# u transposed in pairs on the vector engine and gathered by SBUF copies, in place of TensorE transposes, in a windowed attention followed by a token mixer and an MLP

## The chip, the cores and the metric

The kernel runs on one core of one Trainium2 chip. The metric is device microseconds of one execution. The engines are TensorE (PE; its weight loads are shown as PEld), VectorE (DVE), ScalarE (ACT), GpSimd (POOL) and SyncE (SP). Inputs are float32 in HBM; the kernel works in bfloat16 with float32 sums and returns float32.

## What is computed

```python
def _attn_ref(q, k, v):                      # q, k, v: (8, 8, 576, 64)
    scores = scale * np.matmul(q, k.transpose(0, 1, 3, 2))
    rel = pos[:, None] - pos[None, :]
    mask = (rel >= 0) & (rel < 64)
    scores = np.where(mask, scores, -1000000000.0)
    ...                                      # softmax over the last axis
    return np.matmul(attn, v)

def _moe_ref(x, U, V, w_ch1, w_ch2):         # x: (8, 576, 512), U: (576, 32), V: (32, 576)
    xt = x.transpose(0, 2, 1)
    h = xt @ U @ V
    u = x + h.transpose(0, 2, 1)
    ch = np.maximum(u @ w_ch1, 0.0) @ w_ch2  # 512 -> 2048 -> 512
    return u + ch
```

x is the attention's output with the 8 heads side by side. Per batch the attention, then the low-rank mixing along the sequence, then an MLP for each token.

## The kernel before

The 8 x 576 = 4608 tokens are 36 tiles of 128 tokens. The MLP works on nine chunks of four tiles (512 tokens). The attention and the mixing work by batch (576 tokens, four and a half tiles), so a tile on the border of two batches gets its halves from both.

A hand-written schedule sets the order on every engine. Batch 0 is computed alone at the start. Then, for chunk c, `mlp(c)` gives 32 fills: 16 times `ch1` (four matmuls of 128x512 of the first MLP layer, into PSUM tile `psA`, then a ReLU on ScalarE or, for the five in `DVE_RELU`, on VectorE) and 16 times `ch2` (four matmuls of the second layer into `psU`; every fourth ends a tile, VectorE adds u to give `osb`, and SP's queue stores it). `psA` and `psU` share three PSUM banks. After each fill the work of batch b = c + 1 that is listed for that slot is issued. The lists `PLACE` (batches 3 to 7), `PLACE_1` and `PLACE_2` (batches 1 and 2) give the slots:

- `KT`: VectorE transposes raw Q and K in blocks of 32 (`kt`, `qt`). For batches 0 to 2 it moves pairs of bfloat16 as one 32-bit word; for later batches each element is loaded twice, and single elements are moved. In chunk c they are those of batch b + 1 from batch 3 on.
- `VC`: VectorE copies V shifted by 64 tokens (`vB` from `vA`, `pair_v`).
- `S`: scores of a sixth of the batch (`sc`), Exp on ScalarE (`pts`), the mask on VectorE.
- `PV`: attention times V for one tile (`xr`), normalised by VectorE into `xs`.
- `U`, `V`: the two mixing products. `hh` is copied by ScalarE, `psv` is added to x by VectorE and gives the tile `un` of u.
- `UT`: four TensorE transposes of a tile of u against the identity into a PSUM tile `tpu` (or `tpw`), and one copy into the chunk's transposed tile `uTc`, on ScalarE, for two tiles of batch 1 on VectorE. `uTc` is the moving operand of `ch1`.

For chunk 0 the transposed u is made in PSUM instead (`XT`, `UP`: transposes of x plus the mixing product) and cast by two copies each on ScalarE and VectorE.

`S`, `PV`, `U`, `V` (and `tpw`) take turns in two double PSUM banks (`ps_big`). Loads from HBM are all issued by POOL, in the order of the program: `load_w1`, `load_w2`, `load_kq(b)` (four issues for paired batches, eight for the others), `load_v(b)` (five). POOL is not tied to the chunks: it goes on as soon as the buffers are free. Q and K of batch 4 are issued from slot 5 of chunk 1, those of batches 5 to 7 at the start of chunks 2 to 4, and each needs its raw buffer read by the transposes of two batches before.

Of the kernel before, what the change touches and what calls it, by code (L numbers as in the profile page):

```python
# [8 lines left out]
ACT = mybir.ActivationFunctionType  # L9
ALU = mybir.AluOpType  # L10

BF16 = mybir.dt.bfloat16
FP32 = mybir.dt.float32
# [3 lines left out]
def kernel(  # L17
# [11 lines left out]
    nc = tc.nc  # L29
    B, H, S, D = q.shape  # L30
    DM = H * D
    R = moe_U.shape[1]
    F = moe_w_ch1.shape[1]
    P = nc.NUM_PARTITIONS
# [12 lines left out]
    CH = 512  # L47
# [13 lines left out]
    u_pool = ctx.enter_context(tc.tile_pool(name="un", bufs=14))  # L61
    c1_pool = ctx.enter_context(tc.tile_pool(name="c1", bufs=1))
    wk_pool = ctx.enter_context(tc.tile_pool(name="wk", bufs=2))
    out_pool = ctx.enter_context(tc.tile_pool(name="osb", bufs=4))
    ps_big = ctx.enter_context(tc.tile_pool(name="ps_big", bufs=2, space=bass.MemoryType.PSUM))
    first = ExitStack()
# [8 lines left out]
    NT = 5  # L75
    ident = const.tile([P, P], BF16, name="ident")
    mask = const.tile([P, 2 * NB, W], BF16, name="mask")
    w1b = const.tile([P, NDC, F], BF16, name="w1b")
    w2b = const.tile([P, NFC, DM], BF16, name="w2b")
    ub = [const.tile([P, NT, R], BF16, name=f"ub{i}") for i in range(2)]  # L80
    vrep = const.tile([P, W + S + W], BF16, name="vrep")
    bias = const.tile([P, 12, W], BF16, name="bias")
    idle = const.tile([P, CH], BF16, name="idle")
    xs = [const.tile([P, NT, H, D], BF16, name=f"xs{i}") for i in range(2)]
    vA = [const.tile([P, NFULL, H, VW], BF16, name=f"vA{i}") for i in range(2)]
# [102 lines left out]
    )  # L188
    nc.vector.tensor_copy(out=bias[:, NB:12, :], in_=bias[:, 6:NB, :])

    w1v = moe_w_ch1.rearrange("(c p) n -> p c n", p=P)
    w2v = moe_w_ch2.rearrange("(i p) m -> p i m", p=P)

    def load_w1(lo, hi):
        nc.gpsimd.dma_start(out=w1b[:, :, lo:hi], in_=w1v[:, :, lo:hi])

    def load_w2(lo, hi):
        nc.gpsimd.dma_start(out=w2b[:, lo:hi, :], in_=w2v[:, lo:hi, :])
# [11 lines left out]
    u_tiles = {}  # L210
    uT_tiles = {}

    def uT_of(c):
        if c not in uT_tiles:
            uT_tiles[c] = uT_pool.tile([P, NDC, CH], BF16, name="uTc")
        return uT_tiles[c]


    def attention(b, alone=False):
# [43 lines left out]
        def VC(ts, copy):  # L263
            def f():
                pair_v(b, ts, copy)
            return f
# [174 lines left out]
        def UT(t):  # L441
            def f():
                g = g0 + t
                wide = b == 1 and t % 2 == 1
                if wide:
                    tpb = ps_big.tile([P, 2, 2 * CH], BF16, name="tpw", tag="big")
                    tp = tpb[:, 0, 0:CH].rearrange("p (c q) -> p c q", q=P)
                else:
                    tp = psum["tp"].tile([P, NDC, P], BF16, name="tpu", tag="tp")
                for dc in range(NDC):  # L450
                    nc.tensor.transpose(  # L451
                        tp[:, dc, :], u_tiles[g][:, dc * P : (dc + 1) * P], ident[:]
                    )
                col = (g % TPC) * P
                copy = dve_copy if wide else nc.scalar.copy
                copy(out=uT_of(g // TPC)[:, :, col : col + P], in_=tp[:])  # L456
            return f

        pcs["KT"] = [KT(x, n) for n in range(NJ if pair else NJJ) for x in "kq"]
        pool_copy, dve_copy = nc.gpsimd.tensor_copy, nc.vector.tensor_copy  # L460
        if alone:
            pcs["VC"] = [
                VC(slice(t, t + 1), dve_copy if t < 3 else pool_copy) for t in range(NFULL)
            ]
        else:
            pcs["VC"] = [VC(slice(0, NFULL), dve_copy)]
        pcs["S"] = [SC(n) for n in ((0, 3, 1, 4, 2, 5) if pair else range(NPC))]

        def XT(t):
            def f():  # L470
                for dc in range(NDC):
                    nc.tensor.matmul(
                        xT0[dc // 2][:, dc % 2, t * P : (t + 1) * P],
                        x[:, t, 2 * dc : 2 * dc + 2, :].rearrange("p h d -> p (h d)"),
                        ident[:],
                        start=(t == 0),
                        stop=False,
                    )
            return f

        def UP():
            for dc in (0, 2, 1, 3):
                nc.tensor.matmul(
                    xT0[dc // 2][:, dc % 2, :],
                    hh["sb"][:, dc * P : (dc + 1) * P],
                    vrep[:, W : W + CH],
                    start=False,
                    stop=True,
                )
            for dc in (0, 2, 1, 3):  # L490
                copy = dve_copy if dc // 2 else nc.scalar.copy
                copy(out=uT_of(0)[:, dc, :], in_=xT0[dc // 2][:, dc % 2, :])  # L492

        pcs["XT"] = [XT(t) for t in range(NFULL)]
        pcs["UP"] = UP
        pcs["PV"] = [PV(t) for t in range(NT)]
        pcs["U"] = [UM((t,)) for t in range(NT)] if alone else [UM(tuple(range(NT)))]
        pcs["V"] = [VM((0, 1)), VM((2, 3)), VM((4,))]
        pcs["UT"] = [UT(t) for t in range(NT if odd else NT - 1)]
        return pcs  # L500


    DVE_RELU = (1, 4, 7, 10, 13)

    def mlp(c):
        uTc = uT_of(c)
        c1 = [None] * NFC

        def ch1(i):
            def f():  # L510
                ps = psum["mm"].tile([P, CH], FP32, name="psA", tag="mm")
                for dc in (0, 2, 1, 3) if c == 0 else range(NDC):
                    nc.tensor.matmul(  # L513
                        ps[:],
                        w1b[:, dc, i * P : (i + 1) * P],
                        uTc[:, dc, :],
                        start=(dc == 0),
                        stop=(dc == NDC - 1),
                    )
                c1[i] = c1_pool.tile([P, CH], BF16, name=f"c1_{i}")  # L520
                if i in DVE_RELU:
                    nc.vector.tensor_relu(out=c1[i][:], in_=ps[:])  # L522
                else:
                    nc.scalar.activation(out=c1[i][:], in_=ps[:], func=ACT.Relu)  # L524
            return f

        acc = {}

        def ch2(t, quarter):
            def f():  # L530
                g = c * TPC + t
                if quarter == 0:
                    acc[t] = psum["mm"].tile([P, DM], FP32, name="psU", tag="mm")
                for i in range(4 * quarter, 4 * quarter + 4):
                    nc.tensor.matmul(  # L535
                        acc[t][:],
                        c1[i][:, t * P : (t + 1) * P],
                        w2b[:, i, :],
                        start=(i == 0),
                        stop=(i == NFC - 1),  # L540
                    )
                if quarter == 3:
                    osb = out_pool.tile([P, DM], FP32, name="osb")
                    nc.vector.tensor_tensor(  # L544
                        out=osb[:], in0=acc[t][:], in1=u_tiles[g][:], op=ALU.add
                    )
                    nc.sync.dma_start(out=outf[g * P : (g + 1) * P, :], in_=osb[:])
            return f

        order = [(t, r) for t in range(TPC) for r in range(4)]  # L550
        if c == 0:
            order = [(t, r) for r in range(4) for t in range(3)] + [(3, r) for r in range(4)]
        return [ch1(i) for i in range(NFC)] + [ch2(t, r) for t, r in order]


    PLACE = {
        "VC": [0],
        "S": [1, 1, 4, 4, 7, 7],
        "PV": [10, 10, 13, 13, 15],
        "KT": [8, 9, 11, 12, 14, 15, 16, 18],  # L560
        "U": [17],
        "V": [19, 20, 22],
        "UT": [21, 22, 23, 24, 25],
    }
    PLACE_1 = {
        "KT": [13, 14, 15, 16],
        "S": [16, 16, 18, 18, 20, 20],
        "VC": [21],
        "PV": [23, 23, 25, 25, 26],
        "U": [28],  # L570
        "V": [29, 30, 31],
        "UT": [30, 31, 31, 32, 32],
    }
    PLACE_2 = {
        "KT": [1, 2, 3, 4],
        "S": [5, 5, 8, 8, 11, 11],
        "VC": [9],
        "PV": [14, 14, 16, 16, 18],
        "U": [20],
        "V": [22, 23, 24],  # L580
        "UT": [24, 25, 26, 27, 28],
    }
    KT_3 = [19, 20, 21, 23, 25, 27, 29, 30]
    KT_4 = [11, 12, 14, 16, 18, 19, 22, 25]


    def turn_over(n, cols=CH, to=None):
# [67 lines left out]
    for c in range(NCH):  # L655
# [13 lines left out]
        if b < B:  # L669
            if b == 1:  # L670
                load_kq(2)
            if b + 1 < B:
                load_v(b + 1)
            if b + 2 < B and b > 2:
                load_kq(b + 2)
            if b == 2:
                slots[5].append(lambda: load_kq(4))
            if b == 1:
                slots[23].append(lambda: load_kq(3))
            where = {1: PLACE_1, 2: PLACE_2}.get(b, PLACE)  # L680
            if b <= 2:
                place(b, ("KT",), where)
            place(b, ("VC", "S", "PV"), where)
            if 3 <= b + 1 < B:
                place(b + 1, ("KT",), {2: {"KT": KT_3}, 3: {"KT": KT_4}}.get(b, PLACE))
            place(b, ("U", "V", "UT"), where)
        for fill, extra in zip(mlp(c) + [lambda: None], slots):
            fill()
            for f in extra:
# [31 lines left out]
```

## Time and profile before

| | |
|---|---|
| time, median of 3 runs | 331.26 us (329.37 to 332.1) |
| profiled execution | 330.28 us, its span 328.6 us |
| granted TensorE clock | 0.998 |
| TensorE busy | 318.5 us, 97% of the span, 2949 matmuls |
| VectorE, ScalarE, POOL busy | 195.1, 118.3, 83.0 us |
| transposes of u on TensorE (line 451) | 128, of which 120 into `tpu` |
| copies of `uTc` from them (line 456) | 30 on ScalarE, 586 ns each; 2 on VectorE |
| HBM read, written | 48.94 MB, 9.44 MB |

The span runs from the first to the last instruction; the execution's time is 1.7 us more. A line such as `L451` is line 451 of the kernel. A group of instructions is shown as the output tile, an arrow and the inputs, with count, busy time, mean duration, and the idle time of the engine before it with what ended it. The mean duration of a matmul includes its way through the array; matmuls of 512 columns start 0.216 us apart when they follow each other. In the timeline a line has the start, the busy time, the engine, the line of code, the operation and the number of instructions, and in brackets the idle time before it with what ended it. In tables by stretch, an engine's busy time stands before the number of its instructions.

### The profile page before, as it was taken

The page shows a single profiled execution, that of the slowest core. Times are in us where ns is not written, and L with a number is a line of the kernel's source. Part 1 is how long each engine was busy: PE and PEld are TensorE (multiplying, and loading weights), DVE is VectorE, ACT ScalarE, POOL GpSimd, SP SyncE. Part 2 cuts the span into 40 slices and gives each one's busy share as a digit, 9 for nine tenths or more (in the row PEclk, how much of TensorE's full clock was granted, in tenths as well). Part 3 has the DMA queues.
Part 4 walks back from the last instruction along what each step waited for, and adds up shares of the span by engine and source line. Part 5 has one row for each costly group of instructions (what it writes and reads, how often), then busy time and mean ns, then how long its engine had stood idle before and what let it go on. Part 6 is the DMA issues. An engine that isn't in the chain of part 4 may idle for free.

```text
span 328.6 us, 6914 instructions
## 1 busy us (share of the span) xinstructions
PE 318.5 (97%) x2949; PEld 156.3 (48%) x2949; DVE 195.1 (59%) x339; ACT 118.3 (36%) x188; POOL 83.0 (25%) x112
## 2 busy tenths in 40 slices
PE   8989989899999999999999999999999999999995
PEld 8544444454454545454544454445445444444442
DVE  7654759588787885689457955696456512212211
ACT  1524350365027423552246233732182224203400
POOL 8571419554626226125501400000000000000000
PEclk9999999999999999999999999999999999999999
DMA  7999999999999997999991911001100010021011
GB/s 120 156 199 209 206 137 173 206 197 141 170 189 180 181 111 96 203 105 63 176 225 13 73 64 67 1 2 55 75 2 0 34 66 30 2 89 39 2 64 64
DMA packets 96573, 34.34 MB, mean 105 GB/s; under 512 B 86688, under 2 KB 89888, under 8 KB 96544
## 3 DMA queue, kind: packets, MB, share of 16 engines
q0 software_dynamic: 91360, 24.48, 83.8%
q1 hardware_dynamic: 5184, 9.44, 8.3%
q8 instruction: 23, 0.38, 0.5%
q14 instruction: 6, 0.05, 0.1%
HBM read 48.94 MB, written 9.44 MB: 178 GB/s over the span
## 4 chain that ended last, share of the span: by engine, by line
PE 79%; DMA 12%; DVE 5%; POOL 2%; issue 1%; ACT 0%; DVEq 0%
PE psU L535 36%; PE psA L513 32%; DMA vA<-in_v_dram 7%; DMA kr<-in_k_dram 5%; PE xr L375 3%; PE sc L341 3%; PE psv L420 2%; PE tpu L451 2%; PE pshh L401 1%; DVE un L431 1%; POOL vA L124 1%; DVE xs L385 1%; DVE kt L243 0%; DVE qt L243 0%; DVE osb L544 0%
## 5 line engine op out<-in xcount | busy, mean ns | idle before, releaser
L535 PE MATMUL psU<-w2b,c 128*128 128x512 bf16 x576 | 135.1, 379 | 0.0
L513 PE MATMUL psA<-uTc,w1b 128*128 128x512 bf16 x576 | 131.4, 379 | 0.9 <-DVE uTc L492 0.6
L524 ACT ACTIVATE c<-psA 128x512 bf16<-128x512 f32 x99 | 59.3, 599 | 100.2 <-PE psA L513 99.6
L513 PEld LDWEIGHTS <-w1b 128*128 128x128 bf16 x576 | 53.9, 98 | 63.9 <-issue 1.7
L535 PEld LDWEIGHTS <-c 128*128 128x128 bf16 x576 | 53.6, 98 | 60.2 <-issue 3.0
L544 DVE TENSOR_TENSOR osb<-psU,un 128x512 f32<-128x512 f32 x36 | 24.8, 690 | 64.0 <-PE psU L535 63.9
L522 DVE TENSOR_SCALAR c<-psA 128x512 bf16<-128x512 f32 x45 | 30.8, 685 | 34.8 <-PE psA L513 34.6
L124 POOL DMA_DIRECT2D vA<-in_v_dram x32 | 28.4, 892 | 62.2 <-PE xr L375 19.8
L349 ACT ACTIVATE pts<-sc 128x768 bf16<-128x768 f32 x42 | 31.8, 808 | 11.8 <-PE sc L341 10.0
L456 ACT COPY uTc<-tpu 128x512 bf16<-128x512 bf16 x30 | 17.6, 586 | 40.3 <-PE tpu L451 40.3
L356 DVE TENSOR_TENSOR pts<-pts,mask 128x768 bf16<-128x768 bf16 x42 | 23.1, 557 | 12.2 <-ACT pts L349 9.3
L431 DVE TENSOR_TENSOR un<-psv,xs 128x512 bf16<-128x512 f32 (+1 forms) x40 | 25.7, 682 | 7.0 <-PE psv L420 6.8
L385 DVE TENSOR_TENSOR xs<-xr,rcp 128x512 bf16<-128x512 f32 (+1 forms) x40 | 27.6, 691 | 1.4
L112 POOL DMA_DIRECT2D kr<-in_k_dram x20 | 16.6, 828 | 21.8 <-DVE kt L243 8.8
L375 PEld LDWEIGHTS <-pts 128*64 128x64 bf16 x576 | 12.4, 110 | 10.4 <-DVE xs L385 5.2
L112 POOL DMA_DIRECT2D qr<-in_q_dram x20 | 16.5, 826 | 3.0 <-DMA vA<-in_v_dram 1.1
L243 DVE STREAM_TRANSPOSE kt<-kr 128x576 bf16<-128x576 bf16 x20 | 16.0, 799 | 0.0
L243 DVE STREAM_TRANSPOSE qt<-qr 128x576 bf16<-128x576 bf16 x20 | 15.7, 787 | 0.0
L375 PE MATMUL xr<-vB,pts 128*64 128x65 bf16 x320 | 15.4, 196 | 0.3 <-DVE vB L137 0.2
L341 PEld LDWEIGHTS <-kt 64*64 64x64 bf16 (+1 forms) x720 | 10.1, 105 | 10.8 <-issue 10.4
L410 ACT CAST hh<-pshh 128x512 bf16<-128x512 f32 x8 | 4.7, 586 | 28.9 <-PE pshh L401 28.9
L341 PE MATMUL sc<-qt,kt 64*64 64x128 bf16 (+3 forms) x720 | 12.9, 215 | 1.8 <-issue 1.4
(64 smaller groups left out, 161.8 us busy)
## 6 DMA issues: line engine op xcount, KB each, us to landing
out_dram<-osb SPq DMA_DIRECT2D x36, 256.0 KB, 2.0
kr<-in_k_dram POOLq DMA_DIRECT2D x26, 288.0 KB, 10.4
qr<-in_q_dram POOLq DMA_DIRECT2D x26, 288.0 KB, 11.4
vA<-in_v_dram POOLq DMA_DIRECT2D x32, 128.0 KB, 7.2
w2b<-in_moe_w_ch_dram POOLq DMA_DIRECT2D x2, 1024.0 KB, 19.2
w1b<-in_moe_w_ch_dram POOLq DMA_DIRECT2D x2, 512.0 KB, 9.6
w1b<-in_moe_w_ch_dram POOLq DMA_DIRECT2D x1, 1024.0 KB, 10.6
vB<-in_v_dram POOLq DMA_DIRECT2D x8, 64.0 KB, 7.8
```

Of the source, the lines that this page charges most:

```text
L112: nc.gpsimd.dma_start(out=dst[32 * part : 32 * (part + 1), off : off + NJJ * RD].rearrange("p (n x) -> p n x", x=r * D), in_=src[b, m * NJ ...
L124: nc.gpsimd.dma_start(out=va[:, t, :, 0:D], in_=v[b, :, t * P : (t + 1) * P, :].rearrange("h p d -> p h d"),)
L243: nc.vector.transpose(out=dst[:, n * S : (n + 1) * S].rearrange("q (m p e) -> q m e p", p=32, e=r), in_=src[:, 32 + n * RD : 32 + (n + 1) ...
L341: nc.tensor.matmul(sc[half * W : (half + 1) * W, g, (a - lo) * W : (z - lo) * W], operand("k", g, jj, e, kb * W, (kb + 1) * W), operand("q ...
L349: nc.scalar.activation(out=dst, in_=sc[:, :, 0 : PB * W].rearrange("p g (n w) -> p g n w", w=W), func=ACT.Exp, scale=scale,)
L375: nc.tensor.matmul(xr[r0 : r0 + W, h // 4, (h % 4) * VW : (h % 4 + 1) * VW], pts[:, g, jj * NB + blk, :], rhs, start=True, stop=True,)
L385: nc.vector.tensor_tensor(out=x[lo:hi, t, :, :].rearrange("p (a h) d -> p a h d", a=2), in0=xv[:, :, :, 0:D], in1=rcp[lo:hi].to_broadcast( ...
L431: nc.vector.tensor_tensor(out=u_tiles[g][rs, :], in0=ps[rs, n, :], in1=xt[n][rs], op=ALU.add)
L513: nc.tensor.matmul(ps[:], w1b[:, dc, i * P : (i + 1) * P], uTc[:, dc, :], start=(dc == 0), stop=(dc == NDC - 1),)
L522: nc.vector.tensor_relu(out=c1[i][:], in_=ps[:])
L524: nc.scalar.activation(out=c1[i][:], in_=ps[:], func=ACT.Relu)
L535: nc.tensor.matmul(acc[t][:], c1[i][:, t * P : (t + 1) * P], w2b[:, i, :], start=(i == 0), stop=(i == NFC - 1),)
```

## The change

- For chunks 2 to 8, u is no longer transposed by TensorE. `TR` transposes a tile of u on VectorE, in 32x32 blocks of 32-bit words (pairs of bfloat16), into a staging tile `stg`. `gather` copies `stg` to `uTc` with 16 DMAs of 32 KB from SBUF to SBUF, eight on ScalarE's queue and eight on SP's. Batch 1 keeps `UT` for four tiles (chunk 1).
- `uTc` now holds pairs: contraction index, then token, then the two halves of a pair. So the rows of `w1b` are loaded in that order (two DMAs for each `load_w1`), `ch1` reads every second element of `uTc`, from chunk 2 on in runs of 32 tokens, and `XT`, `UP` and `UT` take every second column of x, `hh` and u.
- Q and K of batches 4 to 7 are loaded by `next_loads`: after the gather of chunk c + 1 (c = 1 to 4) POOL copies one element of each of the last two gathered pieces to `hold`, and then issues `load_kq(c + 3)`.
- V of batch 1 is paired tile by tile (`VC` in four parts).
- The first two `psA` of chunk 0 are taken from `ps_big`.
- The slot lists change: in `PLACE` and `PLACE_2` scores, PV, U and V stand earlier; `KT_4` is gone.

The core of the diff:

```diff
-    w1b = const.tile([P, NDC, F], BF16, name="w1b")
+    w1b = const.tile([P, 2, 2, F], BF16, name="w1b")
+    hold = const.tile([P, 2], BF16, name="hold")
...
     def load_w1(lo, hi):
-        nc.gpsimd.dma_start(out=w1b[:, :, lo:hi], in_=w1v[:, :, lo:hi])
+        for g in range(2):
+            nc.gpsimd.dma_start(out=w1b[:, g, :, lo:hi], in_=w1v[g, :, :, lo:hi])
...
-            uT_tiles[c] = uT_pool.tile([P, NDC, CH], BF16, name="uTc")
+            uT_tiles[c] = uT_pool.tile([P, 2, CH, 2], BF16, name="uTc")
...
-        if alone:
+        if b < 2:
             pcs["VC"] = [
-                VC(slice(t, t + 1), dve_copy if t < 3 else pool_copy) for t in range(NFULL)
+                VC(slice(t, t + 1), pool_copy if alone and t == 3 else dve_copy)
+                for t in range(NFULL)
             ]
...
-        pcs["UT"] = [UT(t) for t in range(NT if odd else NT - 1)]
+        pcs["UT"] = [UT(t) for t in range(NT - 1)] if b == 1 else []
...
+    def TR(g):
+        def f():
+            c, t = divmod(g, TPC)
+            if c not in stages:
+                stages[c] = stg_pool.tile([P, 8, TPC, 32, 2], BF16, name="stg")
+            nc.vector.transpose(
+                out=stages[c][:, :, t, :, :].rearrange("p j q e -> p j (q e)").bitcast(U32),
+                in_=u_tiles[g].bitcast(U32).rearrange("p (j x) -> p j x", x=32),
+            )
...
+    def next_loads(c):
+        def f():
+            for n in (14, 15):
+                i, j = (n + n // 4) % 4, n % 4
+                rows = slice(32 * j, 32 * (j + 1))
+                nc.gpsimd.tensor_copy(
+                    out=hold[rows, 0:1], in_=uT_of(c + 1)[rows, 0, i * TPC * 32, 0:1]
+                )
+            load_kq(c + 3)
...
+    def gather(c):
+        def f():
+            run = TPC * 32
+            for n in range(16):
+                i, j = (n + n // 4) % 4, n % 4
+                queue = nc.sync if n % 2 else nc.scalar
+                queue.dma_start(
+                    out=uT_of(c)[32 * j : 32 * (j + 1), :, i * run : (i + 1) * run, :].rearrange(
+                        "p g n e -> p g (n e)"
+                    ),
+                    in_=stages[c][32 * i : 32 * (i + 1)].rearrange(
+                        "p (g j) t q e -> p g j (t q e)", g=2
+                    )[:, :, j, :],
+                )
...
+        def uT_cols(dc):
+            cols = uTc[:, dc // 2, :, dc % 2]
+            if c < 2:
+                return cols
+            return cols.rearrange("p (i t q) -> p t i q", i=4, t=TPC)
...
+                if c == 0 and i < 2:
+                    ps = ps_big.tile([P, 2, CH], FP32, name="psA0", tag="big")[:, 0, :]
...
     PLACE = {
-        "VC": [0],
-        "S": [1, 1, 4, 4, 7, 7],
-        "PV": [10, 10, 13, 13, 15],
-        "KT": [8, 9, 11, 12, 14, 15, 16, 18],
-        "U": [17],
-        "V": [19, 20, 22],
-        "UT": [21, 22, 23, 24, 25],
+        "VC": [2],
+        "S": [0, 0, 3, 3, 6, 6],
+        "PV": [9, 9, 11, 11, 13],
+        "KT": [14, 15, 16, 17, 22, 23, 25, 26],
+        "U": [15],
+        "V": [17, 18, 20],
     }
     PLACE_1 = {
         "KT": [13, 14, 15, 16],
-        "S": [16, 16, 18, 18, 20, 20],
-        "VC": [21],
-        "PV": [23, 23, 25, 25, 26],
-        "U": [28],
-        "V": [29, 30, 31],
-        "UT": [30, 31, 31, 32, 32],
+        "S": [16, 16, 18, 18, 21, 21],
+        "VC": [20, 21, 22, 23],
+        "PV": [22, 22, 24, 25, 26],
+        "U": [27],
+        "V": [28, 28, 29],
+        "UT": [29, 30, 31, 31],
     }
     PLACE_2 = {
-        "KT": [1, 2, 3, 4],
-        "S": [5, 5, 8, 8, 11, 11],
-        "VC": [9],
-        "PV": [14, 14, 16, 16, 18],
-        "U": [20],
-        "V": [22, 23, 24],
-        "UT": [24, 25, 26, 27, 28],
+        "KT": [0, 0, 1, 2],
+        "S": [2, 2, 5, 5, 8, 8],
+        "VC": [7],
+        "PV": [11, 11, 13, 13, 15],
+        "U": [17],
+        "V": [19, 20, 22],
     }
-    KT_3 = [19, 20, 21, 23, 25, 27, 29, 30]
-    KT_4 = [11, 12, 14, 16, 18, 19, 22, 25]
+    KT_3 = [16, 18, 19, 20, 24, 25, 27, 29]
...
-            if b + 2 < B and b > 2:
-                load_kq(b + 2)
-            if b == 2:
-                slots[5].append(lambda: load_kq(4))
...
+        if 2 <= c + 1 < NCH:
+            g0 = (b * S) // P
+            first = (c + 1) * TPC
+            last = max(first + t - g0 for t in range(TPC)) // 2 if b < B else 0
+            ready = where["V"][last] if b < B else 6
+            for t in range(TPC):
+                slots[ready - 1 + t // 2 if t < TPC - 1 else ready + 1].append(TR(first + t))
+            slots[ready + 1].append(gather(c + 1))
+            if c > 0 and c + 3 < B:
+                slots[ready + 1].append(next_loads(c))
```

In chunk 1 `ready` is slot 20, in chunk 2 slot 18, in chunks 3 to 6 slot 17, in chunk 7 slot 6.

## Prediction

> **What bounds the kernel now.** I read the busy shares first, then the chain, then the groups that the change touches.
>
> ```profile
> PE 318.5 (97%) x2949; PEld 156.3 (48%) x2949; DVE 195.1 (59%) x339; ACT 118.3 (36%) x188; POOL 83.0 (25%) x112
> DMA  7999999999999997999991911001100010021011
> PE psU L535 36%; PE psA L513 32%; DMA vA<-in_v_dram 7%; DMA kr<-in_k_dram 5%; PE xr L375 3%; PE sc L341 3%; PE psv L420 2%; PE tpu L451 2%; PE pshh L401 1%; DVE un L431 1%; POOL vA L124 1%; DVE xs L385 1%; DVE kt L243 0%; DVE qt L243 0%; DVE osb L544 0%
> L456 ACT COPY uTc<-tpu 128x512 bf16<-128x512 bf16 x30 | 17.6, 586 | 40.3 <-PE tpu L451 40.3
> ```
>
> TensorE is the bound: whatever leaves it in the middle of a chunk is gained, as long as nothing else becomes late. VectorE and ScalarE have room. The DMA engines are full for the first 22 slices (180 us) and nearly empty afterwards. The DMA shares of the chain lie in chunk 0, where TensorE was working beside them.
>
> The timeline of chunk 1 gives the price of one transposed tile:
>
> ```profile
> 92.92 1.03 PE L535 MATMUL psU<-w2b,c 128*128 128x512 bf16 x4
> ...
> 93.78 0.39 PE L451 MATMUL tpu<-ident,un 128*128 128x128 bf16 x4
> ...
> 94.00 1.03 PE L535 MATMUL psU<-w2b,c 128*128 128x512 bf16 x4
> ```
>
> Starts count, not durations: four transposes push the next start from 93.78 to 94.00, 0.22 us.
>
> **What is removed.** 28 of 32 groups of four transposes: 27 in chunks 1 to 6, between back-to-back matmuls, 27 x 0.22 = **-5.9 us**; one in chunk 0 (counted there). 28 ScalarE copies of 0.586 us go too, worth nothing by themselves.
>
> **Chunk 0.** Three waits of the old timeline change:
>
> ```profile
> 22.40 1.29 DVE L492 CAST uTc<-xT 128x512 bf16<-128x512 f32 x2 [2.50 <-PE xT L483]
> 23.84 3.40 PE L513 MATMUL psA<-uTc,w1b 128*128 128x512 bf16 x15 [0.61 <-DVE uTc L492]
> ...
> 49.38 0.69 DVE L136 COPY vB<-vA 64x2080 bf16<-64x2080 bf16 x1 [0.30 <-DMA vA<-in_v_dram]
> ```
>
> The first psA waited for all four casts, because its PSUM bank was theirs. In `psA0` it starts at 22.9 with the first cast (ScalarE's, 22.18 plus 0.59); its last matmul waits until 23.77, and the second psA starts at 23.98, not 24.7: -0.7. PV of batch 1 waited for the whole of V; paired by tile, its first two tiles need only the first two loads, which the queue lands about 2 us before the last: -0.4 (the lost starts around 50 us). One transposed tile less: -0.2. At the end V, UT and their copies still run one behind the other on VectorE, and the wider stride of the copies may cost: +0.1. Sum **-1.2**; bounds 0 (the loads of V land later behind three more w1 issues of 0.78 us on POOL's queue; POOL waits 4.7 us for landings there, which covers them, and uncovered they cost up to 0.8) and -1.8.
>
> **What is added, chunks 1 to 6.** Per chunk VectorE gets four transposes. Nearest row, the paired Q/K transposes:
>
> ```profile
> 37.81 1.25 DVE L235 STREAM_TRANSPOSE kt<-kr 128x576 uint32<-128x576 uint32 x1
> 38.90 1.24 DVE L235 STREAM_TRANSPOSE qt<-qr 128x576 uint32<-128x576 uint32 x1
> ```
>
> Start to start 1.085 us for 576 words, so 256 words take 0.48 (0.56 by duration): 13.5 us in all on an engine with 133 us free. What counts is when the last one ends. V of batch 1 in eight small copies of 0.29 instead of two of 0.73 adds 0.9 there, in a part where VectorE waits for loads.
>
> In the built order of the changed kernel, the gather's 16 copies go alternately to ScalarE's and SP's queue, and both share eight completion counters: the ninth copy waits for the first to land. So the gather takes: landing L, then three more issues, then L again. The only rows of these queues are the stores:
>
> ```profile
> L547 SPq DMA_DIRECT2D out_dram<-osb x36: 332/332/362, 53.9 to 325.4; - x36
> DMA to landing us min/median/max: 2.0/2.0/8.0
> out_dram<-osb SPq DMA_DIRECT2D x8, 256.0 KB, 6.7
> ```
>
> Issue 0.33; landing 2.0 on empty engines, 6.7 (median from 50 to 100 us) beside the loads. A store's packets take 84 ns each (8.3% of 16 x 328.6 us over 5184 packets), eight per engine, so 0.7 of its 2.0 is moving; a copy of 32 KB moves an eighth. L lies between 1.4 and 2.0; I take 1.7, so the **gather G = 1.7 + 3 x 0.33 + 1.7 = 4.4** (3.8 to 5.0; beside loads 14). The 112 issues cost SP and ScalarE 18.5 us each: SP waits for store data all the time, and in chunks 1 to 6 ScalarE has nothing between the copy of hh and the next chunk once its uTc copies are gone (it waited 40.3 us for them); stores queued behind a gather leave up to 4 us later, with four buffers behind them. Without that cover it costs what chunk 7 shows below. The Trainium skill, "DMA: Bandwidth & Descriptors", section Bandwidth (Measured), speaks against such copies: under 64 KB descriptors dominate, batch to 1 MiB. Its section Anatomy of one DMA gives 2.0 us plus bytes over 436 GB/s, an estimate of 2.08 for these and 2.6 for the stores, which measured 2.0; by it G is 5.2 and the sum ends 1.2 us higher.
>
> Chunk 1, from its first psA: a slot is 0.865 us, with the blocks of S, PV, U and V between at their old spacing the chunk is 33.7 long (34.8 now, less 4 x 0.22, and a little less stall). VectorE ends the last normalisation at 19.2, two Q/K transposes at 20.6, waits for psU until 22.4, then store addition, transpose, four u additions (0.62 each), four new transposes and one Q/K transpose (0.7): last end 28.9. Landing 28.9 + 4.4 = 33.3: in time by 0.4 us. **0** (0.2 with G 5.0).
>
> Then the moved loads. Q and K of batch 4 to 7 now start after the landing; queued behind them on POOL are V of the same batch and all later loads. Eight DMAs took, in the timeline of POOL and the landings from 153 to 175 us:
>
> ```profile
> 153.86 0.82 POOL L112 DMA_DIRECT2D kr<-in_k_dram  x1 [2.57 <-DVE kt L243]
> ...
> 159.49 0.81 POOL L112 DMA_DIRECT2D qr<-in_q_dram  x1
> ...
> DMA to landing us min/median/max: 7.3/11.0/14.5
> ```
>
> The last issue at 159.49 plus 14.5 is 174.0: 20 us from the first issue, K one landing (2 us) earlier. Batch 5 so loaded was read 25 us later; that reserve is spent. From the gather's landing, at the chunk's start, K is there at 17.9 and Q at 19.9; their transposes stand at slots 14 and 15 (16.5). VectorE waits 3 us; behind are two more of them and the u additions, done at 23.3, while the last V matmul, at 23.24, needs their bank: **+0.1** in chunk 2. With four transposes, two more additions and a store addition behind, the gather there starts at 27.0 and lands at 31.4 of 33.2; the next load is 1.6 us earlier and later chunks lose nothing. V (5.5 us more of transfers) ends at 25.4, just before the gather: this cover is what keeps L small. A round of the loop is 20.2 + 7.1 + G = 31.7 against 33.2.
>
> **Chunk 7.** Here the gather stands at slot 7, among ReLUs. ScalarE runs in order: c_8 waits behind eight issues, four of them behind landings. c1_7 ends at 7.75, the last transpose at 8.35, first landing 10.05, four issues 11.4, c_8 done 12.0. psA 11 needs that bank at 9.5 (three banks): **+2.5** (2.2 to 2.8; nothing if issuing lets ScalarE go on).
>
> **Strided reading.** All 576 psA matmuls now read every second element, in runs of 32. The paired S blocks read so already:
>
> ```profile
> 69.00:69.75 0.75, 0.73 (x48) 0.65 (x48) 1.00 1.82 180
> 100.35:100.80 0.45, 0.44 (x26) 0.39 (x26) 1.00 2.50 113
> ```
>
> These are the windows of line 341. Two strided pieces stream 1536 columns through each quarter of the array in 0.73 us, 0.48 ns a column; two contiguous ones 768 in 0.44, 0.57 ns. At 0.42 ns (216 ns for 512) the bounds are 0 and 0.06 x 512 x 576 = 18 us, but the contiguous row reads no better, so I take **0**. No row has the jumps between runs. On tile choice the skill ("VectorE: DVE Perf Modes", Rules for kernel authors) sends 128x128 transposes to TensorE where PSUM is fine; by that rule alone the gain would be nil, but TensorE is the full engine here.
>
> **Sum.** The profiled run took 330.28 us (span 328.6, 1.7 around it): -5.9 - 1.2 + 0 + 0.1 + 2.5 = -4.5, so 325.8. The median of the runs shown is 331.26, 1.0 above; there it is **326.8 us**, -1.4%. A difference of 1% is about what a measurement here can tell from none.
>
> **Rivals.** *A, the gather is late* (slower). Place: end of chunk 1 and the round of load, transpose, gather. If V's or Q/K's transfers are still running, L rises toward 6.7. Chunk 1 loses G - 4.8, four rounds G - 5.9 each, chunk 7 half of G - 4.4 more. It turns slower from G of about 6.4; with G = 8: 3.2 + 8.4 + 4.3 - 7.1 = +8.8, **340.1**. For: full DMA digits to 180 us and a margin of 0.4. Against: the loads are held back until the landing. *B, nothing is lost*: ScalarE's issues don't block, -7.1, **324.2**. Against: the built order puts the counters' waits on ScalarE. *C, within 1%*: chunk 0 gains nothing and Q/K land some 2 us later than counted, costing about 0.5 in each of four chunks: -5.9 + 2.5 + 2 = -1.4, **329.9**. That the transposes stay is excluded: 16 of 128 are left in the built program.
>
> **How the numbers follow.** Forecast 0.42 (own range 325 to 329), B 0.10, C 0.22, A 0.26. Faster by over 1%: B and most of the forecast, 0.48; within 1%: C and the rest, 0.28; slower, 0.24. The range reaches from B less 1 us to A with G of 7.3: 323.2 to 336.3.
>
> **What would show it.** Right: PE instructions down by 112; gather copies landing near 1.7 us; psA of chunks 2 to 6 starting without a wait; a hole of 2 to 3 us in chunk 7; the psA spacing at 216 ns. Wrong: psA waiting for uTc's copies at chunk starts, Q/K transposes waiting over 4 us for kr and qr, psA over 220 ns.

## The result and the profile after

| | before | after |
|---|---|---|
| time, median | 330.58 us (329.37 to 332.10, 4 runs) | 342.81 us (341.60 to 348.43, 4 runs) |
| ratio | | 1.036 (95% interval 1.029 to 1.042) |
| profiled execution, its span | 330.28, 328.6 us | 342.42, 340.6 us |
| gather of 16 copies, first issue to last landing | | 6.7 to 7.7 us |

One of the four runs after, that of 348.43 us, was in a slower state and is left out of the ratio; without it the median is 342.42, so that the differences from 342.81 below would be 0.4 us smaller.

The forecast was 326.8 us, with a range up to 336.3. The change made the kernel 3.6% slower, so the prediction was wrong in sign and the time lies outside its range. Three lines of the page before (the granted clock in 40 slices, the chain and the group of the first layer) stand first here, and then the same lines after, with the busy times.

```profile
PEclk9999999999999999999999999999999999999999
...
PE 79%; DMA 12%; DVE 5%; POOL 2%; issue 1%; ACT 0%; DVEq 0%
...
L513 PE MATMUL psA<-uTc,w1b 128*128 128x512 bf16 x576 | 131.4, 379 | 0.9 <-DVE uTc L492 0.6
```

```profile
PE 322.6 (95%) x2837; PEld 149.6 (44%) x2837; DVE 204.9 (60%) x373; ACT 101.6 (30%) x160; POOL 87.7 (26%) x123
...
PEclk9999999999999999999999999998999998799999
...
PE 40%; DMA 28%; issue 12%; DVE 8%; POOL 7%; ACTq 4%; ACT 0%; DVEq 0%; POOLq 0%
...
L574 PE MATMUL psA<-uTc,w1b 128*128 128x512 bf16 x576 | 141.1, 392 | 7.2 <-ACT c L585 3.6
```

TensorE has the 112 instructions less that were forecast and is busy 4.1 us *longer*. The mean psA rose from 379 to 392 ns. The clock, at 9 in all slices before, falls in two places. TensorE's share of the chain falls from 79% to 40%; 28% are DMAs now and 12% issues.

The same tables by stretch, cut at the first psA of chunks 1, 4, 5, 7 and 8 (length, then PE, PEld, DVE, ACT, POOL busy, clock, DMA share, GB/s):

```profile
62.80:99.20 36.40, 34.60 (x370) 15.89 (x370) 28.80 (x48) 11.05 (x18) 6.16 (x8) 1.00 1.48 115
...
166.80:200.70 33.90, 33.90 (x291) 15.09 (x290) 25.07 (x44) 11.26 (x18) 10.95 (x15) 1.00 1.65 134
200.70:239.20 38.50, 35.51 (x291) 15.56 (x290) 24.76 (x44) 11.26 (x18) 11.34 (x14) 0.96 1.61 128
...
273.00:308.20 35.20, 30.85 (x130) 12.90 (x129) 7.58 (x13) 6.35 (x11) 0.00 (x0) 0.90 0.14 45
308.20:340.60 32.40, 28.47 (x129) 12.28 (x127) 6.92 (x10) 6.57 (x11) 0.00 (x0) 1.00 0.11 41
```

| chunk | up to 0 | 0 | 1 | 2 | 3 | 4 | 5 | 6 | 7 | 8 | sum |
|---|---|---|---|---|---|---|---|---|---|---|---|
| before | 23.8 | 39.9 | 34.8 | 34.2 | 34.0 | 34.4 | 34.0 | 34.2 | 27.6 | 31.7 | 328.6 |
| after | 22.6 | 40.2 | 36.4 | 33.7 | 33.9 | 33.9 | 38.5 | 33.8 | 35.2 | 32.4 | 340.6 |
| difference | -1.2 | +0.3 | +1.6 | -0.5 | -0.1 | -0.5 | +4.5 | -0.4 | +7.6 | +0.7 | +12.0 |

Four things can be read from it.

**Every psA is slower.** In chunk 8, where no attention runs beside the MLP, there are rows of psA without a gap, one before and one after:

```profile
296.89 4.48 PE L513 MATMUL psA<-uTc,w1b 128*128 128x512 bf16 x20
```

```profile
308.19 5.15 PE L574 MATMUL psA<-uTc,w1b 128*128 128x512 bf16 x22
```

A matmul lasts 0.38 us from start to end, so 20 of them have 19 steps from start to start in 4.10 us, 216 ns each; afterwards 21 steps take 4.77 us, 227 ns. The starts give 226 to 227 ns in all nine chunks, the first two included, where the reading has no runs. Chunk 8 is 0.7 us longer by that alone.

**The gather takes 7 us, and chunk 2 waits for it.** Here are the timeline at the end of chunk 1 and the line of the copies (duration of an issue, min/median/max in ns, and landing):

```profile
91.79 5.21 SPq L546 DMA_DIRECT2D uTc<-stg  x8
91.80 5.54 ACTq L546 DMA_DIRECT2D uTc<-stg  x8
...
98.99 0.43 POOL L533 COPY hold<-uTc 32x1 bf16<-32x1 bf16 x2 [23.81 <-DMA uTc<-stg]
...
99.24 1.06 PE L574 MATMUL psA<-uTc,w1b 128*128 128x512 bf16 x4 [1.83 <-DMA out_dram<-osb]
```

```profile
L546 SPq DMA_DIRECT2D uTc<-stg x56: 585/604/1126, 91.8 to 287.0; - x56
...
DMA to landing us min/median/max: 1.9/1.9/3.4
```

An issue holds its queue for 0.60 us, not 0.33. Each queue spends 5.2 to 5.5 us on its eight copies, and the last one issued lands some 2 us after its issue. TensorE loses 2.0 us of starts: its next matmul starts that much later than one behind the other would. The wait is put down to a store, but POOL's copy to `hold`, which waits for the gather alone, starts 0.25 us before the matmul.

**In chunk 5 Q and K are late.** The timeline there has these rows, three of VectorE and two of TensorE:

```profile
221.25 0.82 DVE L249 STREAM_TRANSPOSE kt<-kr 128x576 bf16<-128x576 bf16 x1 [2.94 <-DMA kr<-in_k_dram]
...
223.84 0.82 DVE L249 STREAM_TRANSPOSE qt<-qr 128x576 bf16<-128x576 bf16 x1 [1.78 <-DMA qr<-in_q_dram]
...
226.55 1.25 DVE L437 TENSOR_TENSOR un<-psv,xs 128x512 bf16<-128x512 f32 x2
...
227.85 0.38 PE L426 MATMUL psv<-hh,vrep 128*128 128x512 bf16 x1 [2.99 <-DVE un L437]
...
228.07 4.22 PE L596 MATMUL psU<-w2b,c 128*128 128x512 bf16 x11
```

VectorE waits 4.7 us for two loads. The additions of u stand behind them, and the third `psv` needs the bank that these additions free. TensorE loses 3.15 us of starts. Of the matmuls that follow, eight start 427 ns apart: that is half the clock, and another 1.7 us.

**In chunk 7 ScalarE stands behind its issues.**

```profile
281.52 6.23 ACTq L546 DMA_DIRECT2D uTc<-stg  x8
...
287.86 1.57 ACT L585 ACTIVATE c<-psA 128x512 bf16<-128x512 f32 x3 [7.70 <-DMA uTc<-stg]
288.50 6.04 PE L574 MATMUL psA<-uTc,w1b 128*128 128x512 bf16 x16 [3.57 <-ACT c L585]
```

Three ReLUs come late, and TensorE loses 0.94 and 3.73 us. Then the clock is halved: the next 12 steps of psA take 4.97 us in place of 2.72, so 2.25 us more.

### The profile page after: what moved, and what is told of

The parts are those of the page before. It is cut to its first block, busy times and chain, and to the rows that moved or that the text cites. A ratio compares the mean times of both kernels' runs of the same rounds, so it can differ in the third digit from the quotient of the medians.

```text
span 340.6 us, 6859 instructions
## 1 busy us (share of the span) xinstructions
PE 322.6 (95%) x2837; PEld 149.6 (44%) x2837; DVE 204.9 (60%) x373; ACT 101.6 (30%) x160; POOL 87.7 (26%) x123
## 4 chain that ended last, share of the span: by engine, by line
PE 40%; DMA 28%; issue 12%; DVE 8%; POOL 7%; ACTq 4%; ACT 0%; DVEq 0%; POOLq 0%
PE psU L596 19%; PE psA L574 17%; DMA vA<-in_v_dram 15%; DMA qr<-in_q_dram 9%; ACTq L546 4%; DMA w1b<-in_moe_w_ch_dram 3%; POOL kr L114 3%; POOL qr L114 2%; DVE un L437 2%; PE sc L347 1%; DMA uTc<-stg 1%; DVE xs L391 1%; DVE osb L605 1%; DVE qt L249 1%; POOL vA L126 1%
## 5 line engine op out<-in xcount | busy, mean ns | idle before, releaser
L574 PE MATMUL psA<-uTc,w1b 128*128 128x512 bf16 x576 | 141.1, 392 | 7.2 <-ACT c L585 3.6
L596 PE MATMUL psU<-w2b,c 128*128 128x512 bf16 x576 | 132.5, 383 | 0.0
L596 PEld LDWEIGHTS <-c 128*128 128x128 bf16 x576 | 55.4, 98 | 72.9 <-issue 9.8
L574 PEld LDWEIGHTS <-w1b 128*128 128x128 bf16 x576 | 52.9, 97 | 77.1 <-issue 10.7
L391 DVE TENSOR_TENSOR xs<-xr,rcp 128x512 bf16<-128x512 f32 (+1 forms) x40 | 27.6, 691 | 1.4
L533 POOL COPY hold<-uTc 32x1 bf16<-32x1 bf16 x8 | 1.5, 184 | 78.8 <-DMA uTc<-stg 78.5
L114 POOL DMA_DIRECT2D qr<-in_q_dram x20 | 17.5, 874 | 2.6 <-DMA vA<-in_v_dram 1.6
L426 PE MATMUL psv<-hh,vrep 128*128 128x512 bf16 x40 | 12.4, 379 | 3.2 <-DVE un L437 3.2
```

What stands on the lines that cost most here:

```text
L114: nc.gpsimd.dma_start(out=dst[32 * part : 32 * (part + 1), off : off + NJJ * RD].rearrange("p (n x) -> p n x", x=r * D), in_=src[b, m * NJ ...
L391: nc.vector.tensor_tensor(out=x[lo:hi, t, :, :].rearrange("p (a h) d -> p a h d", a=2), in0=xv[:, :, :, 0:D], in1=rcp[lo:hi].to_broadcast( ...
L574: nc.tensor.matmul(ps if c < 2 else ps.rearrange("p (t i q) -> p t i q", i=4, t=TPC), w1b[:, dc // 2, dc % 2, i * P : (i + 1) * P], uT_col ...
L596: nc.tensor.matmul(acc[t][:], c1[i][:, t * P : (t + 1) * P], w2b[:, i, :], start=(i == 0), stop=(i == NFC - 1),)
```

## The experiments

Twelve kernels were run. Times are medians; ratios are against the kernel before on the same chip (330.3 to 330.5 us). Gathers, starts and waits are read from each kernel's own trace.

### Strided reading alone

This is the kernel before, with `uTc` in pairs:

```diff
-            uT_tiles[c] = uT_pool.tile([P, NDC, CH], BF16, name="uTc")
+            uT_tiles[c] = uT_pool.tile([P, 2, CH, 2], BF16, name="uTc")
...
-                        uTc[:, dc, :],
+                        uTc[:, dc // 2, :, dc % 2],
```

> The kernel before, with uTc stored in pairs as the changed kernel stores it and read by psA at every second element; the TensorE transposes, the slots and the loads stay, and there is no gather. Theory S (every strided psA matmul costs 227 ns start to start in place of 216, as the traces of after and before show): 576 x 0.011 = +6.3 us, so 336.9 against 330.6, ratio 1.019, with the psA spacing at 227 ns. By the prediction's term (strided reading costs 0): 330.6 and 216 ns. If the 11 ns come from the runs of 32 tokens or from the loads of w1b by halves, which this kernel has not, also 330.6.

The kernel took 337.31 us, ratio 1.020 (1.017 to 1.023), so +6.5 us (5.6 to 7.5). One stretch of its psA reads:

```profile
309.74 4.47 PE L516 MATMUL psA<-uTc,w1b 128*128 128x512 bf16 x19
```

These are 18 steps in 4.09 us, 227 ns each. The price of the stride is shown, without a gather, without runs of 32 and without loads of `w1b` in halves. The Trainium skill, "SBUF — State Buffer", on cachelines, counts strides of up to 8 bf16 as free; here the second element already costs 5%, and the measurement decides.

### The changed kernel with contiguous reading

```diff
-            cols = uTc[:, dc // 2, :, dc % 2]
...
+            half = dc % 2
+            return uTc[:, dc // 2, half * (CH // 2) : (half + 1) * (CH // 2), :].rearrange(
+                "p q e -> p (q e)"
+            )
```

> The changed kernel, whose psA matmuls read contiguous halves of the same uTc in place of every second element (so they multiply other elements; everything else is as it was). Theory S: -6.3, so 336.5 against 342.8, ratio to the kernel before 1.018; up to 1.5 us less of a gain where a chunk waits for loads anyway (chunk 5). Rival (the spacing is set by the clock or by the copies that run beside): 342.8 and still 227 ns.

The kernel took 338.43 us, ratio 1.023 (1.017 to 1.030), 4.4 less than the changed kernel, and psA is at 216 ns. The rival falls by the spacing; the intervals of the two ratios, some 2 us to each side, leave open how much of the 6.3 the time shows. Part of it may go back into waits: this trace has holes (stretches without a start of a matmul) of 3.0, 1.6 and 5.2 us in chunks 3, 5 and 7, 9.8 in all, where the changed kernel's chunks 3 to 7 have 8.2.

### The last gather on SP's queue

```diff
-                queue = nc.sync if n % 2 else nc.scalar
+                queue = nc.sync if n % 2 or c == NCH - 1 else nc.scalar
```

> The changed kernel with all 16 copies of the last gather (in chunk 7) on SP's queue; the other gathers are unchanged. Theory B (ScalarE's ReLUs stand behind its eight issues, and the hole slows TensorE's clock afterwards): the hole of 4.7 us and the slow matmuls behind it (2.5 us) go, 342.8 - 7.1 = 335.7; the last copy lands by 294, before chunk 8. Rival (the hole is a wait for landings that any queue would have, or DVE's): 342.8. Of the issue: if one copy costs its queue 0.6 us, the 16 take 9.6 us; if two queues share one unit at 0.3 us a copy, 16 on one queue take about 5 us.

The kernel took 335.46 us, ratio 1.013 (1.008 to 1.019): 7.35 less than the changed kernel, as theory B expected. In chunk 7 the timeline reads:

```profile
279.75 7.87 PE L574 MATMUL psA<-uTc,w1b 128*128 128x512 bf16 x34
...
281.59 11.02 SPq L546 DMA_DIRECT2D uTc<-stg  x16
```

There are 34 matmuls without a break where the changed kernel had both holes, and the clock of the stretch is 1.00. One queue alone issues a copy every 0.64 us, the same as each of two: the queues don't share the 0.6.

### Q and K loaded a chunk earlier

The calls of `next_loads` are taken out, and `load_kq(4)` to `load_kq(7)` stand where the kernel before had them.

> The changed kernel with Q and K of batches 4 to 7 issued where the kernel before issued them, a chunk earlier, without the copies to hold. Theory L (chunk 5 loses 4.9 us because Q and K of batch 7, which start only behind the gather, land 23 us later while their transposes stand ahead of u on VectorE): chunk 5 loses nothing, -4.9; the gather of chunk 1 then runs beside loads and may land later, 0 to +4: 338 to 342. Rival (loads beside the gathers are worse than late loads): gathers take over 10 us in several chunks and the time is 343 or more.

The kernel took 357.55 us, ratio 1.083 (1.076 to 1.089). Theory L's half came, since no psv waits in chunk 5 any more; but the time is that of the rival, far above its 343. The gather of chunk 1, beside the loads, takes 19.6 us (its copies land after 6.4 to 10.7), that of chunk 2 takes 10.7, and TensorE stands before chunks 2 and 3 for 14.5 and 2.7 us:

```profile
L574 PE MATMUL psA<-uTc,w1b 128*128 128x512 bf16 x571 | 143.7, 399 | 21.9 <-DMA uTc<-stg 16.9
```

So holding the loads back is what keeps the landings at 1.9 us; the prediction had this right.

### One run per partition

`stg` and `uTc` are laid out so that a copy is 1 KB in one piece for each partition.

```diff
-                stages[c] = stg_pool.tile([P, 8, TPC, 32, 2], BF16, name="stg")
+                stages[c] = stg_pool.tile([P, 4, 2, TPC, 32, 2], BF16, name="stg")
```

> The changed kernel with stg and uTc laid out so that each of the 16 copies is one contiguous run of 1 KB per partition on both sides (two runs of 512 B before); psA still reads every second element. Theory I (the issue of 0.6 us a copy, where the stores take 0.33, comes from the shape of the copy): issues at 0.33, a gather of 4.4 to 5 us in place of 6.7 to 7.5; the wait of 2.0 us at the end of chunk 1 goes, Q and K land 2 us earlier (another -3 in chunks 3 to 5, with the slow clock behind), and chunk 7 loses about 2.5 in place of 7.1: together 332 to 334. Rival (a copy from SBUF to SBUF costs 0.6 us of its queue whatever its runs): 0.6 again and 342 to 343.

The kernel took 341.54 us, ratio 1.034 (1.027 to 1.040), with issues of 0.60 us and gathers of 6.6 to 7.4. Theory I falls: it is not the runs that make an issue cost 0.6 us.

### Transposes of Q and K late

```diff
-        "KT": [14, 15, 16, 17, 22, 23, 25, 26],
+        "KT": [19, 20, 21, 22, 24, 25, 27, 28],
```

> The changed kernel with the eight transposes of Q and K at slots 19 to 28 (in PLACE) in place of 14 to 26, so that on VectorE the additions of u and the new transposes stand ahead of them. Theory L (VectorE waits for kr and qr in front of u; the late u stops psv and TensorE for 3.5 us in all in chunks 3 to 5 and its clock halves behind the longest stop, 1.7 us): these 5.2 us go, the gathers start without VectorE's wait: 337 to 338. Rival (the transposes are then too late for the next chunk's scores, or u is late for another reason): 342 or more, with waits of sc for kt or qt at chunk starts.

The kernel took 337.13 us, ratio 1.020 (1.016 to 1.023): 5.7 less than the changed kernel. The wait of psv for `un`, 3.2 us there, is down to 0.2 in its list of waits, and the gathers of chunks 3 to 5 start 1.5 to 4.6 us sooner, counted from their chunk's first psA. Theory L holds. The wait at the end of chunk 1 stays (1.85 us of starts), and this kernel's list of waits puts it down to the gather by name.

### Holes of known length

This is the kernel before with six holes made on TensorE in chunks 7 and 8.

```diff
+    def hole(n):
+        to = fresh()
+        nc.tensor.matmul(to[:, 0, :], idle[:, 0:P], idle[:], start=True, stop=True)
+        for _ in range(n):
+            nc.vector.tensor_relu(out=idle[:], in_=to[:, 0, :])
+        nc.tensor.matmul(fresh()[:, 0, 0:W], idle[:, 0:P], idle[:, 0:W], start=True, stop=True)
```

> The kernel before with six holes made on TensorE in chunks 7 and 8, where nothing else is due: a matmul, then 2, 3, 4, 5, 6 and 8 VectorE operations of some 0.69 us on its result, then a matmul that reads theirs; so holes of about 1.7, 2.4, 3.1, 3.8, 4.5 and 5.8 us, 21 in sum. Theory C (a hole of over about 3 us is followed by matmuls at half the clock, 427 ns apart for some 3.4 us, a further 1.7 us lost; the changed kernel shows it behind holes of 3.2 and 3.7 us and not behind one of 2.0): four of the six are followed by it: 330.6 + 21 + 6.8 = 358. By the Trainium skill, TensorE: Matmul & The Clock Gate, part on the clock gate, an idle window of about 3.4 us that runs freely lowers the clock; then 3.1 and 3.8 may pass without, depending on where they fall: 355 to 358. Rival (the clock fell in the changed kernel for another reason, such as ScalarE's or the DMAs' work beside it): 216 ns behind every hole, 351.6.

| lost starts, us | 2.06 | 2.40 | 3.13 | 4.24 | 4.58 | 6.03 |
|---|---|---|---|---|---|---|
| matmuls at half the clock behind it | 0 | 8 | 0 | 11 | 8 | 13 |

The rows of psU behind the second and the third hole read:

```profile
290.83 8.76 PE L535 MATMUL psU<-w2b,c 128*128 128x512 bf16 x31
...
302.81 1.46 PE L535 MATMUL psU<-w2b,c 128*128 128x512 bf16 x6
```

Behind the second, 30 steps take 8.38 us, 279 ns each on average, where 5 steps after the *longer* third hole take 1.08 us, 216 ns each. The kernel took 363.84 us in its one run: 22.4 us of holes, 40 slow matmuls at 0.211 more each (8.4) and twelve added matmuls account for 32.4 of the 33.3 us above the kernel before. The rival falls: idleness alone lowers the clock. The rule "over 3 us" falls too; 2.4 can be enough and 3.1 can pass.

The clock's own record settles why. In each of the 14 traces the granted clock changes only at times that lie whole multiples of 3.41 us apart, so that the time falls into fixed stretches of 3.41 us; where they begin differs from one execution to the next. Cut at these borders, the profile of this kernel reads:

| stretch, us | 273.80 to 277.21 | 287.45 to 290.86 | 297.69 to 301.10 | 301.11 to 304.51 | 311.35 to 314.75 |
|---|---|---|---|---|---|
| what lies in it | the hole of 2.06 | the hole of 2.40 | the first part of that of 3.13 | the rest of it | most of that of 4.24 |
| TensorE busy, us | 1.52 | 1.17 | 2.12 | 1.74 | 1.33 |
| clock of the next stretch | 1.00 | 0.50 | 1.00 | 1.00 | 0.50 |

The same holds in all 14 traces, from 20 us on: each of the 22 stretches at full clock in which TensorE was busy for up to 39% is followed by one at half the clock, and none of the 1250 with 44% or more. So the hole of 3.13 passed because it lay across a border, and a hole of that length can pass in one execution and cost 1.7 us in another. That fits the free-running window of the Trainium skill, "TensorE: Matmul & The Clock Gate", part on the clock gate; its limit of about 3.4 us for a gap doesn't hold for the hole of 2.4.

### Single elements in place of pairs

`TR` transposes bf16 elements, not 32-bit pairs; `uTc`, `w1b`, `XT`, `UP` and `UT` are as in the kernel before.

```diff
-                out=stages[c][:, :, t, :, :].rearrange("p j q e -> p j (q e)").bitcast(U32),
-                in_=u_tiles[g].bitcast(U32).rearrange("p (j x) -> p j x", x=32),
+                out=stages[c][:, :, t, :],
+                in_=u_tiles[g].rearrange("p (j x) -> p j x", x=32),
```

> The changed kernel with u transposed on VectorE by single elements, not pairs, so that uTc and w1b have the layout of the kernel before and psA reads contiguous elements in runs of 32; the gather's copies have four runs of 256 B per partition. Theory S (stride, not the jump between runs, costs the 11 ns): psA at 216 ns, -6.3. VectorE's transposes take about 0.70 in place of 0.42 us (0.79 for 576 columns in the trace), so the gathers start 0.3 to 1.1 us later: +1 to +2 in chunk 1 and in the rounds of the loads. 336.5 to 339. Rival (the jumps cost as well): still above 220 ns, 342 or more. If the issue grows with the number of runs (theory I), gathers of over 9 us and 342 or more too, but with psA at 216 ns.

The kernel took 343.56 us, ratio 1.038 (1.034 to 1.043). psA is at 216 ns with the runs of 32, so the jumps cost nothing; the copies, in four runs now, still issue in 0.61 to 0.62 us, and the gathers take 6.8 to 7.3 us (the last 8.4). But the expected 336.5 to 339 was missed: a transpose takes 0.69 us, waits of 3.2 and 1.2 us stand before chunks 2 and 3, and psv lost 5.8 us in chunks 3 and 4, with a slow clock behind the longest wait. VectorE is late already, and 0.27 us more, four times a chunk, seems to have cost more than was allowed for; no run takes this apart from the other waits.

### The mends together, in pairs and in single elements

Both kernels have the late transposes as above (in chunk 1 at slots 23 to 30, the edit shown) and the last gather on SP; the second has single elements besides.

```diff
-    KT_3 = [16, 18, 19, 20, 24, 25, 27, 29]
+    KT_3 = [23, 24, 25, 26, 27, 28, 29, 30]
```

> The changed kernel with three mends: the transposes of Q and K late in every chunk (slots 19 to 28, in chunk 1 slots 23 to 30), and the last gather on SP's queue alone. The strided reading stays. If the losses found so far are separate and add up: 342.8 - 5.7 (late loads, as the run of that alone showed) - 7.3 (last gather, as the run of that alone showed) - 1.8 (the wait at the end of chunk 1, since VectorE now gives u there some 3 us earlier) = 328.0, ratio 0.992. If they overlap, or the wait at the end of chunk 1 has another cause (the gather's own 7 us from a u that TensorE itself gives late): 330 to 331.

The kernel in pairs took 329.80 us, ratio 0.998 (0.997 to 1.000): 13.0 less than the changed kernel, and 1.8 less of a gain than if the parts added up in full. The wait before chunk 2 went from 2.0 to 0.8, not to 0.

> The kernel of the mended pairs, with u transposed by single elements, so that psA reads contiguous elements at 216 ns: 6.3 us less than that, less some 0.5 where the longer transposes (0.68 in place of 0.42 us) still delay a gather: 322 to 323, ratio 0.976 to the kernel before, -2.4%. If the longer transposes bring back the waits at chunk ends: 326 to 329.

The kernel in single elements took 325.97 us, ratio 0.987 (0.985 to 0.989), the fastest of all, 1.3% below the kernel before. The expected 322 to 323 was missed by some 3 us. Waits of 1.65 and 0.63 us before chunks 2 and 3 (the first put down to a transpose of Q) are 1.5 more than in pairs; the rest isn't accounted for. Its psA in chunk 8 reads:

```profile
292.24 7.93 PE L568 MATMUL psA<-uTc,w1b 128*128 128x512 bf16 x36
```

These are 35 steps in 7.55 us, 216 ns each. Chunks 3 to 6 take 33.0 to 33.1 us here, where those of the kernel before take 34.0 to 34.4.

### Chunk 0 alone

This is the kernel before with `psA0`, V of batch 1 by tile and the new slots of `PLACE_1`:

```diff
+                if c == 0 and i < 2:
+                    ps = ps_big.tile([P, 2, CH], FP32, name="psA0", tag="big")[:, 0, :]
```

> The kernel before with the change's edits to chunk 0 alone: the first two psA from ps_big, V of batch 1 paired by tile, the slots of PLACE_1 as changed (with its fifth transposed tile kept). By the prediction -0.7 for the first psA and -0.4 for PV, less 0.1 at the end of the chunk: 329.5, ratio 0.997. Rival (the loads set chunk 0, and what is gained at its start is waited for at its end): 330.5, ratio 1.000.

The kernel took 329.50 us, ratio 0.997 (0.995 to 0.999), so -1.1 us (-1.8 to -0.4), against the -1.0 of the prediction.

### What an issue costs

> The kernel before with extra copies on SP's queue in chunk 7, whose results nothing reads, four of each: A, 32 KB from 32 partitions of SBUF to 32 others, as in the gather; B, 128 KB between all 128 partitions; C, 32 KB between all 128 partitions; D, 32 KB from HBM to 32 partitions. And F: in chunk 8 the first two tiles are stored in four stores of 32 partitions each. Theory D (the 0.6 us of an issue belong to copies with SBUF on both sides): A, B and C near 0.60, D and F near 0.33. Rival P (it belongs to copies of 32 partitions): A, D and F near 0.60, B and C near 0.33. The time stays at 330.5.

The kernel took 329.74 us in its one run. Here are the copies A to D, by their line:

```profile
L619 SPq DMA_DIRECT2D toA<-w2b x4: 575/586/617, 269.9 to 271.8; - x4
L619 SPq DMA_DIRECT2D toB<-w2b x4: 591/599/600, 272.4 to 274.4; - x4
L619 SPq DMA_DIRECT2D toC<-w2b x4: 599/599/600, 275.0 to 276.9; - x4
L619 SPq DMA_DIRECT2D toD<-in_q_dram x4: 409/420/587, 277.6 to 279.1; - x4
```

An issue takes 0.59 to 0.60 us from SBUF to SBUF, whether 32 or 128 KB, from 32 or 128 partitions. It takes 0.42 from HBM after a first of 0.59, and 0.32 to 0.43 for the stores of 32 partitions. Theory D holds in the main (its 0.33 for D was too low): it is having both ends in SBUF that costs 0.6. Size doesn't; it shows in the landing alone, 2.1 us for 128 KB and 1.8 for 32 KB.

## Why the prediction was wrong

**What it had right.** The removed transposes are worth what was said: with the waits mended, chunks 2 to 6 of the single-element kernel are 5.4 us shorter (its wait of 0.63 taken out) for 23 groups, 0.23 each against 0.22. The first psA starts at 22.60 (22.9 was forecast), and chunk 0 gave -1.1 for the part tried. From the first issue to the last landing Q and K took 19.4, 19.8 and 20.1 us in chunks 2 to 4 (20). The VectorE transposes take 0.42 us (0.48 was the estimate), landings 1.9 (1.7), and ScalarE does block behind its issues.

**Strided reading, taken as 0: the largest term that failed.** It costs 6.5 us, inside the bounds of 0 to 18, but no rival and no end of the range was built on them. The value came from blocks of scores, 48 pieces of 64 to 192 columns on 32 rows and 64 columns of the array each, beside 26 contiguous ones on 64 rows. A column took 0.48 ns in the strided and 0.57 ns in the contiguous ones; at that rate a cost of 0.02 ns a column can't be seen. The nearest row was the wrong size. This term alone turns -4.5 into +2.

**The gather, G = 4.4 with 3.8 to 5.0.** It measured 6.7 to 7.7. The landing was right; the issue of 0.33 was taken from stores, and a copy within SBUF takes 0.60. The form of the sum fell with it: not two landings and three issues, but eight issues 0.64 apart on each queue and one landing, 7.0. A queue needs some 2.5 us for its first four copies, so the first landing is past when the ninth copy's turn comes, and the counters hardly bind. The estimate by the Trainium skill, "DMA: Bandwidth & Descriptors", section Anatomy of one DMA (2.08 a copy, G = 5.2), was nearer, but it took the same issues, and that section describes DMAs issued by GpSimd, where these are issued by SP and ScalarE. By rival A's rule a G of 5.2 adds 0.4 in chunk 1 and 0.4 in chunk 7, so 0.8 and not the 1.2 that the prediction gives.

**Three waits follow from the long gather,** by the price rule that rival A stated. Chunk 1 loses G - 4.8 = 2.3 (measured 2.0; forecast 0). The round of the loop is 20.2 + 7.1 + 6.75 = 34.05 against chunks of 33.9, not 31.7 against 33.2, so that any late landing goes straight into TensorE: four rounds at G - 5.9 = 0.85 make 3.4 (measured 3.5, nearly all in chunk 5, where Q landed 22.8 us after the first issue, not 20.1; in other runs chunks 3 and 4 pay). Chunk 7 loses 2.5 + 3.3 / 2 = 4.15 (measured 4.7; forecast 2.5).

**The clock had no term at all.** Two holes above 3 us cost 1.7 and 2.25 us behind them.

The sum with the measured terms is -5.9 - 1.2 + 6.3 + 2.0 + 3.5 + 4.7 + 3.9 = +13.3, against the +12.0 between the two profiled spans; some 1.3 us of it stay unassigned. Rival A, at 0.26, had the places of the waits and their price right, but by the issue, not by its stated cause (landings that rise to 6.7 beside running transfers). With the gathers as measured its rule gives 2.3 + 3.4 + 4.15 - 7.1 = +2.75; the rest is the stride and the clock, which no rival had. The signs of being wrong that the prediction named all came: psA waits for the copies, Q's and K's transposes wait 4.7 us, and psA is at 227 ns.

## What to carry to other kernels

- Price a changed operand by a row of the same size: a matmul of 512 columns has to be timed as one. Where none exists, the full bound belongs in the range.
- Take the cost of a DMA issue from a copy with the same two ends, and set it beside the queue's other work: eight of them held back three ReLUs.
- On an engine that works in order, work that waits for a load goes behind work that doesn't.
- A hole of more than two microseconds on TensorE can have a second price: here 1.7 to 2.7 us more (8 to 13 matmuls at half the clock), or nothing, by where it fell.

## What the runs showed of the hardware

- A matmul whose bf16 moving operand is read at every second element starts every 227 ns for 512 columns in place of 216, with or without jumps between runs of 32; the jumps alone cost nothing (216 ns).
- An issue of a copy from SBUF to SBUF holds SP's or ScalarE's queue for 0.60 us, whatever its size, partitions or runs; 0.33 to 0.42 where one end is HBM.
- Holes of 2.40 us and of 4.2 us and more halved the clock for 8 to 13 matmuls; one of 3.13 did not. The clock changes only on a grid of 3.41 us; a stretch of it with TensorE busy for up to 39% was followed by half the clock, and one with 44% or more never was.
